# Attention and two gated layers in one kernel: token tiles of 4, 2, 4, 4, 4 blocks in place of 4, 3, 4, 4, 3

## The chip, the cores and the metric

One NeuronCore of a Trainium2 chip runs the kernel. The metric is the device time of one execution in microseconds, taken as the median of several runs.

## What is computed

A windowed attention (4 sequences of 576 tokens, 8 heads of 64, each token sees itself and the 63 before it) gives 2304 tokens of 512 values. Two gated layers follow, each with a hidden width of 1536; all is float32.

```python
scores = scale * np.matmul(q, k.transpose(0, 1, 3, 2))
mask = (rel >= 0) & (rel < window)
...
x = np.ascontiguousarray(attn_out.transpose(0, 2, 1, 3)).reshape(B * S, H * D)
# first layer
g = x @ w_gate
silu = g * (1.0 / (1.0 + np.exp(-g)))
x = silu * (x @ w_val) @ w_out
# second layer
gate = 1.0 / (1.0 + np.exp(-(x @ w_gate)))
out = gate * (x @ w_val) @ w_out
```

## The kernel before, in words

The 2304 tokens are 18 **blocks** of 128. Blocks are grouped into five **token tiles** (`BLOCKS`, L63); before, they hold 4, 3, 4, 4 and 3 blocks, so 512, 384, 512, 512 and 384 columns.

**The start.** The attention of the blocks of tile 0 (blocks 0 to 3) is done first, in an order written out by hand: `LOADS` (L23) is the order of the loads on SyncE's queue, `START` (L27) the order of the steps. A step has two letters and a block number. `tq`/`tk` transpose a block's queries and keys on TensorE, `eq`/`ek` copy them out, `se`/`so` make the scores of the even and the odd heads, `me`/`mo` mask them on VectorE, `xe`/`xo` are the exponentials on ScalarE, `ne`/`no` normalise on VectorE, `pe`/`po` transpose the result on TensorE, `we`/`wo` copy it out on ScalarE, `vp` copies value rows on GpSimd, `pv` multiplies by the values, `hi`/`lo` split the result into two float32r parts. `ca`, `cb`, `ch`, `cl` are the four parts of converting one piece of 512 KB of the first layer's weights (`ca`, `ch` on ScalarE, `cb`, `cl` on VectorE); `mn` makes a mask; `wm` are matmuls on zeros. `SPLIT_EARLY` (L34) counts the pieces converted in the start; the others are converted in the main loop.

**The main loop.** For each tile and each of the 12 slices `fc` of the hidden width there are three **steps** `g` (L1083 to L1113): twelve matmuls for the gate (`product`, bank `g`), twelve for the values (bank `v`), and twelve (`out_product`) that multiply the slice before by its output weights into the banks `a0` to `a3`. A tile thus has 36 steps, and every matmul has as many columns as its tile. Gate, product and split of the hidden slice are on ScalarE (L1092, L1101) and VectorE (L1099, L1015).

**Work put between the steps.** Three tables (`before`, `during`, `after`, L475) say for each step which other work is issued there. `plan_attention` (L492) puts the attention of block `i` around a step `base`: the scores at `base + 2`, masks and exponentials at `base + 2` and `base + 3`, normalisation at 4 or 5, the transposes of the result at 7 to 9, and the values' product either two steps later in a bank of its own (`att`, two buffers) or together with the next block's scores in bank `g`. Up to block 7 (`TURN` is 8) queries and keys are transposed on TensorE (`transpose_in`, L191); from block 8 on they are loaded in pieces of 32 rows by 32 (`load_squares`, L130: queries from SyncE's queue, keys from GpSimd's) and turned on VectorE (`turn`, L220).

In the same way `operands` (L588) prepares the weights of the second layer from step `starts[n]` on (L660), and `reload` (L409) brings back the output weights of the first layer, seven steps ahead of their use, into one of three buffers (L580). After a tile, `finish` (L459) copies the four banks into tiles of the pool `t` (seven buffers) and stores them.

After the five tiles, the second layer runs in three pairs of 384 columns with fewer products (`strassen`, `outs`); the change does not touch it.

Of the kernel before, what the change touches and what calls it, by code (L numbers as in the profile page):

```python
# [8 lines left out]
FP32 = mybir.dt.float32  # L9
# [11 lines left out]


LOADS = """  # L23
k0 q0 q1 k2 k1 q2 r1 v3 q3 r2 v0 v1 k3 h0 r3 v2
"""

START = """  # L27
tk0 tq0 tq1 ek0 eq0 se0 eq1 so0 tk2 tk1 me0 mo0 ek1 xe0 ne0 tq2 xo0 so1 mo1 eq2 ca0 ek2 se1 no0
so2 se2 xo1 ma0 vp0 ca1 me1 xe1 pe0 mb0 mo2 po0 no1 cb0 xo2 me2 wm2 tk3 ne1 tq3 no2 ek3 ch0 wo0
po1 we0 pe1 ca2 eq3 wo1 so3 vp1 se3 cb1 xe2 mo3 me3 we1 po2 pv0 hi0 xe3 vp2 xo3 ne2 ch1 vp3 wo2  # L30
pv1 pe2 lo0 cl0 ne3 cb2 hi1 we2 lo1 wm2 wm1 wm2 pe3 no3 ca3 cb3 ca4 pv2 hi2 po3 we3 wm3 lo2 wo3
cb4 pv3 wm1 mn0 hi3 ca5 ch3 ch4 lo3 cb5 ch2 ch5 cl4 cl1 cl2 cl5 cl3
"""
SPLIT_EARLY = START.count("ca")  # L34


@with_exitstack
def attention_moe_moe(
# [21 lines left out]
    HP = H // 2  # L60
    W = 64
    scale = 1.0 / float(D) ** 0.5
    BLOCKS = [4, 3, 4, 4, 3]  # L63
    NTL = len(BLOCKS)
    N2 = 384
    PAIRS = NT // (2 * N2)
    JJ = FC // 2
    assert NT == PAIRS * 2 * N2
    TURN = BLOCKS[0] + BLOCKS[1] + 1
    TILES = []  # L70
    t0 = 0
    for n in BLOCKS:
# [177 lines left out]
                    stop=True,  # L250
                )

    def p_tile(tag, name):
        if early[0]:
            return w_p.tile([128, HP, 128], FP32, tag="g", name=name)
        return p_p.tile([128, HP, 128], FP32, tag=tag, name=name)

    def masked(i, par):
        ps = st.pop((i, "s", par))
        z = p_tile(f"z{par}", f"z{par}")  # L260
# [13 lines left out]
        st[i, "z", par] = z, nm  # L274
# [36 lines left out]

    def evacuate_p(i, par):
        ps = st.pop((i, "pp", par))
        t = p_tile(("pt0", "z0")[par], f"pt{par}")
        nc.scalar.activation(out=t, in_=ps, func=ACTF.Copy)
        st[i, "pt", par] = t

# [16 lines left out]
    def x_hi(i, xt, col):  # L334
        nc.scalar.activation(out=xt[:, 0, :, col:col + 128], in_=st[i, "x"], func=ACTF.Copy)  # L335
# [120 lines left out]

    x1d = [dram.tile([128, CC, N2], FP32, name=f"x1d{j}") for j in range(2 * PAIRS)]

    def finish(acc, t, n, parts=range(CC)):  # L459
        for e in parts:  # L460
# [22 lines left out]
    def at(where, g, fn, *a, first=False):  # L483
        where.setdefault(g, []).append((not first, fn, a))
# [7 lines left out]
    def plan_attention(i, base, t, col):  # L492
        if t == 1:
            turn_at, pv_at = (7, 8), 9 if col == 256 else 10
        elif t == 2:
            turn_at, pv_at = (8, 8), 10
        elif col == 0:
            turn_at, pv_at = (8, 9), 10
        else:
            turn_at, pv_at = (7, 8), 9  # L500
        if i >= TURN:
            lead = 9 if i > TURN else 8
            for j in range(4 * HP):
                at(during, base - lead + j * (lead - 3) // (4 * HP), load_squares, i, "kq"[j % 2], j // 4, j // 2 % 2)
        elif base >= 2:
            at(during, base - 5, load_qk, i)
        at(during, base + 1 if i < TURN else base - 2, load_v, i)
        at(during, base + 5 if i <= TURN else base + 2, load_before, i)
        for nm in "qk":
            if i < TURN:  # L510
                at(before, base + 1, transpose_in, i, nm)
                at(before, base + 1, evacuate, i, nm)
            else:
                at(during, base - 1, turn, i, nm, first=nm == "k")
        place[i] = t, col
        if i >= TURN:
# [5 lines left out]
        at(after, base + 2, masked, i, 0, first=True)  # L522
        at(after, base + 3, masked, i, 1, first=True)
        at(after, base + 3, exps, i, 0, first=True)
        at(after, base + 3, exps, i, 1, first=True)
        at(after, base + (4 if i < TURN else 5), normalize, i, 0, first=i >= TURN)
        at(after, base + 5, normalize, i, 1, first=True)
        for par in range(2):
            at(before, base + turn_at[par], transpose_p, i, par)
            at(before, base + turn_at[par], evacuate_p, i, par)  # L530
        if TURN - 1 <= i < NT // 128 - 1:
            return
        at(before, base + pv_at, pv, i)
        at(before, base + pv_at, lambda: x_hi(i, x_of(t), col))
        if t == 1 and col < 256:
            at(before, base + pv_at + 1, lambda: x_lo(i, x_of(t), col))
        else:
            at(during, base + pv_at, lambda: x_lo(i, x_of(t), col), first=True)


    blk = BLOCKS[0]
    for t in range(NTL - 1):
        nb = BLOCKS[t + 1]
        for b in range(nb):
            plan_attention(blk + b, SPT * t + {4: 9 * b - 3, 3: 12 * b - (3 if t else 0), 2: 18 * b + 3}[nb], t + 1, b * 128)
        blk += nb


# [470 lines left out]
    with tc.manual_schedule():  # L1019
# [14 lines left out]
        for step in LOADS.split():  # L1034
# [138 lines left out]
```

## Time and profile before

| | |
|---|---|
| median of 3 runs | 938.1 us (937.07 to 939.4) |
| the profiled execution's own time | 939.13 us |
| its span | 937.4 us, mean granted TensorE clock 0.994 |
| TensorE, matmuls | busy 922.1 us, 98% |
| VectorE | busy 695.1 us, 74% |
| ScalarE | busy 475.4 us, 51% |
| GpSimd | busy 208.3 us, 22% |

Busy is the share of the span in which an engine works on at least one instruction. Matmuls overlap, so the rate of a run of matmuls is read from the start of one group to the start of the next, not from the mean duration. 1.7 us of the execution's time lie outside the span.

### The profile page before, as it was taken

Reading aid. Unit: us, or ns where it says so; the run is one execution under the profiler, and the core shown is the slowest. Engines: PE = TensorE matmul, PEld = TensorE weight load, DVE = VectorE, ACT = ScalarE, POOL = GpSimd, SP = SyncE. Lnnn points to the kernel's source line nnn. Section 1 sums busy time; section 2 is a strip of 40 time slices with the busy share of each in tenths; the row PEclk is TensorE's granted clock in tenths of the full one; section 3 lists DMA queues with packets and bytes.
Section 4 is the critical chain, followed back from the end, with each engine's and each line's share of the span. In section 5 each row is a group of like instructions: output and inputs, shape, how many; then the busy total and the mean of one; then the engine's idle time right before and its main releaser. Section 6 shows DMA issues by size and latency. Waiting matters only on the chain.

```text
span 937.4 us, 17091 instructions
## 1 busy us (share of the span) xinstructions
PE 922.1 (98%) x5933; PEld 841.8 (90%) x5933; DVE 695.1 (74%) x1614; ACT 475.4 (51%) x1079; POOL 208.3 (22%) x368
## 2 busy tenths in 40 slices
PE   7899999999999999999999999999999999999998
PEld 6688888999887888888899999999899999999987
DVE  6899996677666757676655578789677889678795
ACT  6898985666656556546433332246212247122342
POOL 3301015555585616331311000000200000100001
PEclk8999999999999999999999999999999999999999
DMA  9688767888869868786699468738987828978555
GB/s 219 185 247 263 248 223 228 243 238 248 255 206 287 264 216 264 238 276 217 234 324 378 161 224 304 245 146 280 367 306 267 309 90 288 400 239 289 206 181 201
DMA packets 172565, 234.45 MB, mean 250 GB/s; under 512 B 71648, under 2 KB 104800, under 8 KB 172480
## 3 DMA queue, kind: packets, MB, share of 16 engines
q1 hardware_dynamic: 149904, 179.21, 60.0%
q0 software_dynamic: 18256, 45.50, 13.7%
q10 hardware_dynamic: 4320, 8.65, 2.5%
q8 instruction: 47, 0.77, 0.3%
q14 instruction: 38, 0.31, 0.1%
HBM read 184.55 MB, written 48.76 MB: 249 GB/s over the span
## 4 chain that ended last, share of the span: by engine, by line
PE 87%; DMA 4%; ACT 3%; DVE 2%; POOL 2%; SPq 1%; issue 1%; ACTq 0%; POOLq 0%
PE g L438 14%; PE a L449 14%; PE v L438 14%; PE a L793 13%; PE a L944 9%; PE att L793 7%; PE g L793 4%; PE v L793 4%; PE att L944 2%; DMA k<-in_k_dram 2%; PE att L245 1%; DMA wop<-wd 1%; POOL k L136 1%; PE g L325 1%; PE att L309 1%
## 5 line engine op out<-in xcount | busy, mean ns | idle before, releaser
L449 PE MATMUL a<-h,wo 128*128 128x512 f32 (+1 forms) x720 | 161.2, 372 | 0.0
L438 PE MATMUL v<-x,wv 128*128 128x512 f32 (+1 forms) x720 | 159.2, 369 | 0.0
L438 PE MATMUL g<-x,wg 128*128 128x512 f32 (+1 forms) x720 | 158.8, 369 | 0.4 <-ACT x L335 0.3
L438 PEld LDWEIGHTS g<-x,wg 128*128 128x128 f32 x720 | 131.0, 188 | 18.2 <-ACT x L335 0.6
L449 PEld LDWEIGHTS a<-h,wo 128*128 128x128 f32 x720 | 129.6, 188 | 18.5 <-issue 2.2
L438 PEld LDWEIGHTS v<-x,wv 128*128 128x128 f32 x720 | 130.3, 188 | 16.2
L793 PE MATMUL a<-xs,wop 128*128 128x384 f32 x720 | 130.2, 334 | 0.6 <-DMA wop<-wd 0.5
L793 PEld LDWEIGHTS a<-xs,wop 128*128 128x128 f32 x720 | 125.1, 188 | 1.4 <-PE a L793 1.1
L944 PE MATMUL a<-w,hs 128*128 128x256 f32 (+1 forms) x666 | 113.6, 306 | 0.0
L136 POOL DMA_DIRECT2D k<-in_k_dram x176 | 101.9, 585 | 40.9 <-PE att L195 22.3
L934 POOL DMA_DIRECT2D out_dram<-o x33 | 17.8, 541 | 372.8 <-DVE o L915 372.8
L944 PEld LDWEIGHTS a<-w,hs 128*128 128x128 f32 x666 | 93.6, 190 | 6.4
L1099 DVE TENSOR_TENSOR s<-s,v 128x512 f32<-128x512 f32 (+1 forms) x60 | 37.9, 632 | 78.8 <-PE v L438 58.1
L785 ACT ACTIVATE s<-s 128x384 f32<-128x384 f32 x72 | 37.9, 526 | 76.9 <-DVE s L779 75.7
L793 PE MATMUL att<-xs,wop 128*128 128x384 f32 x396 | 73.9, 334 | 0.0
L1092 ACT ACTIVATE s<-g 128x512 f32<-128x512 f32 (+1 forms) x60 | 33.2, 553 | 74.3 <-PE g L438 74.1
L793 PEld LDWEIGHTS att<-xs,wop 128*128 128x128 f32 x396 | 69.0, 188 | 0.0
L1101 ACT ACTIVATE h<-s 128x512 fp32r<-128x512 f32 (+1 forms) x60 | 35.1, 586 | 62.0 <-DVE s L1099 61.7
L633 POOL DMA_DIRECT2D wd<-stage x48 | 31.9, 665 | 136.3 <-DVE stage L619 117.5
L96 DVE TENSOR_TENSOR hs<-hid,hs 128x384 fp32r<-128x384 f32 x108 | 55.3, 551 | 7.3 <-ACT hs L95 7.3
L95 ACT ACTIVATE hs<-hid 128x384 fp32r<-128x384 f32 x108 | 51.3, 520 | 15.0 <-DVE hid L783 11.4
L282 ACT ACTIVATE z<-z,nm 128x128 f32<-128x128 f32 x144 | 55.8, 389 | 1.0 <-DVE nm L264 0.9
(159 smaller groups left out, 1477.6 us busy)
## 6 DMA issues: line engine op xcount, KB each, us to landing
wop<-wd SPq DMA_DIRECT2D x126, 512.0 KB, 6.8
w<-wdo SPq DMA_DIRECT2D x63, 512.0 KB, 5.7
wo<-k0o SPq DMA_DIRECT2D x48, 512.0 KB, 5.3
wd<-stage POOLq DMA_DIRECT2D x36, 512.0 KB, 5.6
raw<-in_moe_w_gate_dram SPq DMA_DIRECT2D x24, 512.0 KB, 4.5
raw<-in_moe_w_val_dram SPq DMA_DIRECT2D x24, 512.0 KB, 4.3
raw<-in_moe_w_out_dram SPq DMA_DIRECT2D x24, 512.0 KB, 4.9
wdo<-stage POOLq DMA_DIRECT2D x18, 512.0 KB, 5.7
```

Of the source, the lines that this page charges most:

```text
L95: nc.scalar.activation(out=dst_hi, in_=src, func=ACTF.Copy)
L96: nc.vector.tensor_tensor(out=dst_lo, in0=src, in1=dst_hi.bitcast(FP32), op=ALU.subtract)
L136: eng.dma_start(out=nat[i, nm][r0:r0 + 32, c, off // 32:(off + m) // 32], in_=src[b, 2 * c + par, s:s + m, 32 * a:32 * a + 32].rearrange(" ...
L282: nc.scalar.activation(out=z[:, hp, :], in_=z[:, hp, :], func=ACTF.Exp, scale=-1.0, bias=nm[:, hp:hp + 1], accum_out=su[:, hp:hp + 1],)
L438: nc.tensor.matmul(out=ps[:, 0:n], lhsT=w[:, a, c, :], rhs=xt[:, b, c, 0:n], start=(j == 0), stop=(j == len(mm) - 1),)
L449: nc.tensor.matmul(out=acc[e][:, 0:n], lhsT=w[:, a, e * 128:(e + 1) * 128], rhs=h[:, b, 0:n], start=(fc == 0 and j == 0), stop=(fc == FC - ...
L785: nc.scalar.activation(out=to[which], in_=to[which], func=ACTF.Sigmoid)
L793: nc.tensor.matmul(out=ps, lhsT=w[:, val, a, c, :], rhs=xops[op, b][:, c], start=(n == 0), stop=(n == len(mm) - 1),)
L944: nc.tensor.matmul(out=acc[e] if both else acc[e][:, 0:256], lhsT=h[a][:, e * 128:(e + 1) * 128], rhs=w.rearrange("p s f -> p (s f)") if b ...
L1092: nc.scalar.activation(out=s, in_=gps[:, 0:n], func=ACTF.Silu)
L1099: nc.vector.tensor_tensor(out=s, in0=s, in1=vps[:, 0:n], op=ALU.mult)
L1101: nc.scalar.activation(out=h[:, 0, 0:n], in_=s, func=ACTF.Copy)
```

## The change

The tiles now hold 4, 2, 4, 4, 4 blocks: 512, 256, 512, 512, 512 columns. The blocks of attention are placed by a table with a row for each block from 4 on: base, the steps of the two transposes, of the values' product and of the lower part of the split. `TURN` falls from 8 to 7, so block 7 is now loaded in squares and turned on VectorE; a new `JOIN` (10) is the block from which values' products go together with the next block's scores, which was from block 7 on before. For blocks 7 and 9 the softmax tiles come from the pool `t`. `finish` copies all four banks in one step, where before two were copied one step later. Two pieces of weights fewer are converted in the start (four for six). The start's values' products alternate between the bank `a2` and the pool `att`.

```diff
-k0 q0 q1 k2 k1 q2 r1 v3 q3 r2 v0 v1 k3 h0 r3 v2
+q0 k0 q1 k1 k2 q2 r1 v0 q3 r2 k3 r3 v3 v1 v2 h0
...
-tk0 tq0 tq1 ek0 eq0 se0 eq1 so0 tk2 tk1 me0 mo0 ek1 xe0 ne0 tq2 xo0 so1 mo1 eq2 ca0 ek2 se1 no0
...
+tq0 tk0 ek0 eq0 se0 tq1 eq1 so0 tk1 me0 tk2 mo0 ek1 xe0 ne0 so1 tq2 xo0 mo1 eq2 ek2 se1 so2 ma0
...
+PLAN = [
+    (0, 11, 11, 13, 15),
+    (15, 22, 23, 25, 27),
+    (27, 37, 37, 39, 39),
+    (39, 47, 47, 51, 51),
+    (48, 55, 55, 57, 58),
+    (57, 65, 65, 67, 67),
...
-    BLOCKS = [4, 3, 4, 4, 3]
+    BLOCKS = [4, 2, 4, 4, 4]
...
+    JOIN = sum(BLOCKS[0:3])
...
+        if BLOCKS[0] + BLOCKS[1] <= i <= JOIN and (i - BLOCKS[0]) % 2:
+            return t_p.tile([128, HP, 128], FP32, tag="t", name=name)
...
-        if i >= TURN:
+        if i > JOIN:
             t1, col1 = place[i - 1]
             at(before, base + 2, pv, i - 1, "g")
...
-        at(after, base + (4 if i < TURN else 5), normalize, i, 0, first=i >= TURN)
-        at(after, base + 5, normalize, i, 1, first=True)
+        at(after, base + (2 + 3 if mid else 4 if i < TURN else 5), normalize, i, 0, first=mid or i >= TURN)
+        at(after, base + (2 + 3 if mid else 5), normalize, i, 1, first=True)
...
-    starts = [39, 48, 58, 66, 75, 81, 87, 93, 100, 107, 114, 120, 126, 132, 138, 145, 155, 161]
+    starts = [43, 58, 72, 78, 84, 89, 94, 101, 106, 111, 117, 123, 129, 135, 141, 147, 153, 161]
...
-            "pv": lambda i: pv(i, "a2"),
+            "pv": lambda i: pv(i, ("a2", None)[i % 2]),
...
-                    finish(*done, parts=(0, 1))
-                    at(during, g + 1, finish, *done, (2, 3))
+                    finish(*done)
```

Two places in the order of the instructions. The first is VectorE in the start, up to the last normalisation of block 3. Before (`z_488` and `z_482` are block 3's even and odd heads, `raw`/`t` a weight conversion, `x<-a` the lower part of a split):

```order
L338 TENSOR_TENSOR x<-a_501,x 128x4x128
L424 TENSOR_TENSOR wg<-t,wg 128x512
L295 TENSOR_SCALAR su<-su 128x4
L296 RECIPROCAL su<-su 128x4
L301 TENSOR_TENSOR z_488<-z_488,su 128x512
L398 TENSOR_SCALAR raw<-raw 128x512
L399 TENSOR_SCALAR t<-t 128x512
L400 ISA t<-raw,t 128x1024
L338 TENSOR_TENSOR x<-a_542,x 128x4x128
L295 TENSOR_SCALAR su<-su 128x4
L296 RECIPROCAL su<-su 128x4
L301 TENSOR_TENSOR z_482<-z_482,su 128x512
```

The same place with the change (here `z_482` is the odd and `z_498` the even half of block 3):

```order
L314 TENSOR_SCALAR su<-su 128x4
L315 RECIPROCAL su<-su 128x4
L320 TENSOR_TENSOR z_482<-z_482,su 128x512
L443 TENSOR_TENSOR wg<-t,wg 128x512
L314 TENSOR_SCALAR su<-su 128x4
L315 RECIPROCAL su<-su 128x4
L320 TENSOR_TENSOR z_498<-z_498,su 128x512
L357 TENSOR_TENSOR x<-a_504,x 128x4x128
L417 TENSOR_SCALAR raw<-raw 128x512
L418 TENSOR_SCALAR t<-t 128x512
L419 ISA t<-raw,t 128x1024
L357 TENSOR_TENSOR x<-att,x 128x4x128
```

One conversion and two lower parts of splits have moved from ahead of the last normalisation to behind it.

The second is SyncE's queue of loads in the start. Before, from the sixth load on (the first key row is that of block 3):

```order
L111 DMA q<-in_q_dram 128x8x64
L371 DMA raw<-in_moe_w_gate_dram 128x4x256
L371 DMA raw<-in_moe_w_val_dram 128x4x256
L111 DMA v<-in_v_dram 128x8x64
L111 DMA q<-in_q_dram 128x8x64
L371 DMA raw<-in_moe_w_gate_dram 128x4x256
L111 DMA v<-in_v_dram 128x8x64 x2
L111 DMA k<-in_k_dram 128x8x64
L111 DMA q<-in_q_dram 64x8x64 x2
```

With the change:

```order
L128 DMA q<-in_q_dram 128x8x64
L390 DMA raw<-in_moe_w_gate_dram 128x4x256
L390 DMA raw<-in_moe_w_val_dram 128x4x256
L128 DMA v<-in_v_dram 128x8x64
L128 DMA q<-in_q_dram 128x8x64
L390 DMA raw<-in_moe_w_gate_dram 128x4x256
L128 DMA k<-in_k_dram 128x8x64
L390 DMA raw<-in_moe_w_val_dram 128x4x256
L128 DMA v<-in_v_dram 128x8x64 x3
```

The keys of block 3 have moved ahead of two loads of values, 256 KB each; the other values, and the loads for block 4, follow later.

## Rows read from the trace of the kernel before

**Rows 1.** Windows of tiles 0 and 1: length, busy by engine, clock, DMA share, GB/s
```profile
39.86:150.81 110.95, 110.95 (x700) 90.57 (x701) 102.55 (x232) 95.27 (x194) 17.96 (x25) 1.00 0.76 239
150.81:239.78 88.97, 88.84 (x722) 85.90 (x721) 62.40 (x175) 58.16 (x142) 48.58 (x87) 1.00 0.85 247
```

**Rows 2.** TensorE's waits from 40 to 535 us: total, times, longest
```profile
PE g L325 <- ACT s L1092: 1.4, 1, 1.4
```

**Rows 3.** Timeline of TensorE: start, length, what; the first product of tile 0
```profile
39.86 3.04 PE L438 MATMUL g<-x,wg 128*128 128x512 f32 x12 [0.26 <-ACT x L335]
```

**Rows 4.** Timeline of VectorE in the start: conversions, a lower part, the last normalisation
```profile
23.32 1.13 DVE L398 TENSOR_SCALAR raw<-raw 128x512 uint16<-128x512 uint16 x1
...
25.24 0.69 DVE L400 CUSTOM_DVE_ANT_0 t<-raw,t 128x1024 uint16<-128x1024 uint16 x1
...
31.96 0.79 DVE L398 TENSOR_SCALAR raw<-raw 128x512 uint16<-128x512 uint16 x1
...
33.93 0.68 DVE L338 TENSOR_TENSOR x<-a,x 128x512 fp32r<-128x512 f32 x1
...
34.94 0.69 DVE L301 TENSOR_TENSOR z<-z,su 128x512 f32<-128x512 f32 x1
35.55 0.75 DVE L398 TENSOR_SCALAR raw<-raw 128x512 uint16<-128x512 uint16 x1
...
36.58 0.69 DVE L400 CUSTOM_DVE_ANT_0 t<-raw,t 128x1024 uint16<-128x1024 uint16 x1
```

**Rows 5.** The chain of waits in the start: start, length, what
```profile
14.42 7.03 DMA k<-in_k_dram
```

**Rows 6.** The page: rate of all transfers in 40 equal slices of the span
```profile
GB/s 219 185 247 263 248 223 228 243 238 248 255 206 287 264 216 264 238 276 217 234 324 378 161 224 304 245 146 280 367 306 267 309 90 288 400 239 289 206 181 201
```

**Rows 7.** Timeline of TensorE: groups of matmuls of 512, 384 and 256 columns
```profile
50.36 2.88 PE L438 MATMUL v<-x,wv 128*128 128x512 f32 x12
53.08 2.88 PE L449 MATMUL a<-h,wo 128*128 128x512 f32 x12
...
200.03 2.24 PE L449 MATMUL a<-h,wo 128*128 128x384 f32 x12
202.11 2.24 PE L438 MATMUL g<-x,wg 128*128 128x384 f32 x12
...
623.88 6.84 PE L944 MATMUL a<-w,hs 128*128 128x256 f32 x55
630.56 0.40 PE L944 MATMUL g<-w,hs 128*128 128x512 f32 x1
```

**Rows 8.** Timeline of TensorE: transposes of one block's queries and keys, and what follows
```profile
42.74 0.60 PE L195 MATMUL att<-ident,q 128*128 128x128 f32 x4
...
43.53 2.98 PE L438 MATMUL v<-x,wv 128*128 128x512 f32 x12
```

**Rows 9.** Tile 1, groups by line: issuing key squares from GpSimd, count, busy, mean ns
```profile
L136 POOL DMA_DIRECT2D k<-in_k_dram x63 | 36.6, 587 | 9.0 <-DMA wdo<-stage 3.4 <-DVE kt L227 2.7 <-DMA k<-in_k_dram 1.6
```

**Rows 10.** Timelines: lower part of hidden slice 1 (VectorE), output product of that slice (TensorE)
```profile
60.09 0.69 DVE L1015 TENSOR_TENSOR h<-s,h 128x512 fp32r<-128x512 f32 x1
...
62.08 3.02 PE L449 MATMUL a<-h,wo 128*128 128x512 f32 x12
```

**Rows 11.** Tile 1: a reload's issue on SyncE, its output product, landing times of output weights
```profile
217.50 0.42 SPq L411 DMA_DIRECT2D wo<-k0o x1
...
229.02 2.33 PE L449 MATMUL a<-h,wo 128*128 128x384 f32 x12
...
wo<-k0o SPq DMA_DIRECT2D x48, 512.0 KB, 5.3
DMA to landing us min/median/max: 3.1/5.3/8.7
```

**Rows 12.** Tile 1, waits of SyncE's queue: total, times, longest
```profile
SPq L371 <- DMA wdo<-stage: 24.3, 4, 8.0
```

**Rows 13.** Timeline of GpSimd in the start: a copy of value rows
```profile
23.90 1.02 POOL L148 COPY v<-v 64x512 f32<-64x512 f32 x1
```

More of the change, by code (lines that the diff above doesn't have):

```diff
@@ L23 @@
 LOADS = """
-k0 q0 q1 k2 k1 q2 r1 v3 q3 r2 v0 v1 k3 h0 r3 v2
+q0 k0 q1 k1 k2 q2 r1 v0 q3 r2 k3 r3 v3 v1 v2 h0
 """
 START = """
-tk0 tq0 tq1 ek0 eq0 se0 eq1 so0 tk2 tk1 me0 mo0 ek1 xe0 ne0 tq2 xo0 so1 mo1 eq2 ca0 ek2 se1 no0
[L29 to L32, printed above, removed]
-"""
+tq0 tk0 ek0 eq0 se0 tq1 eq1 so0 tk1 me0 tk2 mo0 ek1 xe0 ne0 so1 tq2 xo0 mo1 eq2 ek2 se1 so2 ma0
+xo1 se2 ca0 vp0 ca1 me1 no0 po0 no1 pe0 mo2 mb0 xo2 me2 wm2 cb0 we0 xe1 tq3 tk3 no2 ne1 ek3 xe2
+wo0 po1 eq3 pe1 ca2 wo1 so3 ch0 vp1 se3 cb1 mo3 we1 po2 ne2 me3 pv0 xo3 vp2 pe2 vp3 pv1 xe3 wm2
+wo2 hi0 no3 we2 wm3 po3 cl0 ne3 pe3 lo0 pv2 hi1 wo3 ch1 cb2 we3 hi2 pv3 ca3 mn0 lo1 lo2 hi3 cb3
+lo3 ch2 cl1 ch3 cl3 cl2
+"""
+PLAN = [
[5 more added lines that the diff above has]
+    (57, 65, 65, 67, 67),
+    (69, 78, 78, 80, 80),
+    (78, 86, 86, 88, 88),
+    (87, 95, 95, 97, 99),
+    (96, 104, 104, 105, 105),
+    (105, 113, 113, 115, 115),
+    (114, 123, 123, 126, 126),
+    (123, 133, 133, 135, 135),
+    (132, 141, 141, 143, 143),
+]
 SPLIT_EARLY = START.count("ca")
@@ L259, in masked @@
         ps = st.pop((i, "s", par))
-        z = p_tile(f"z{par}", f"z{par}")
+        z = p_tile(i, f"z{par}", f"z{par}")
         nm = sm_p.tile([128, HP], FP32, tag=f"nm{par}", name=f"nm{par}")
@@ L313, in evacuate_p @@
         ps = st.pop((i, "pp", par))
-        t = p_tile(("pt0", "z0")[par], f"pt{par}")
+        t = p_tile(i, ("pt0", "z0")[par], f"pt{par}")
         nc.scalar.activation(out=t, in_=ps, func=ACTF.Copy)
@@ L457, in attention_moe_moe, with finish @@
     x1d = [dram.tile([128, CC, N2], FP32, name=f"x1d{j}") for j in range(2 * PAIRS)]
-    def finish(acc, t, n, parts=range(CC)):
-        for e in parts:
+    def finish(acc, t, n):
+        for e in range(CC):
             o = t_p.tile([128, 512], FP32, tag="t", name="o")
@@ L490, in attention_moe_moe, with plan_attention @@
     place = {}
[L492 to L500, printed above, removed]
+    def plan_attention(i, t, col):
+        base, p0, p1, pv_at, lo_at = PLAN[i - BLOCKS[0]]
         if i >= TURN:
-            lead = 9 if i > TURN else 8
+            lead = max(base - 9, PLAN[i - BLOCKS[0] - 1][0])
             for j in range(4 * HP):
-                at(during, base - lead + j * (lead - 3) // (4 * HP), load_squares, i, "kq"[j % 2], j // 4, j // 2 % 2)
+                at(during, lead + j * (base - 3 - lead) // (4 * HP), load_squares, i, "kq"[j % 2], j // 4, j // 2 % 2)
         elif base >= 2:
@@ L521, in plan_attention @@
         at(before, base + 2, scores, i)
[L522 to L525, printed above, removed]
-        at(after, base + (4 if i < TURN else 5), normalize, i, 0, first=i >= TURN)
-        at(after, base + 5, normalize, i, 1, first=True)
+        mid = BLOCKS[0] + BLOCKS[1] <= i < JOIN
+        at(after, base + (2 + 0 if mid else 2), masked, i, 0, first=True)
+        at(after, base + (2 + 1 if mid else 3), masked, i, 1, first=True)
+        at(after, base + (2 + 1 if mid else 3), exps, i, 0, first=True)
+        at(after, base + (2 + 1 if mid else 3), exps, i, 1, first=True)
+        at(after, base + (2 + 3 if mid else 4 if i < TURN else 5), normalize, i, 0, first=mid or i >= TURN)
+        at(after, base + (2 + 3 if mid else 5), normalize, i, 1, first=True)
         for par in range(2):
-            at(before, base + turn_at[par], transpose_p, i, par)
-            at(before, base + turn_at[par], evacuate_p, i, par)
-        if TURN - 1 <= i < NT // 128 - 1:
+            at(before, (p0, p1)[par], transpose_p, i, par)
+            at(before, (p0, p1)[par], evacuate_p, i, par)
+        if JOIN <= i < NT // 128 - 1:
             return
[L533 to L536, printed above, removed]
+        at(before, pv_at, pv, i)
+        at(before, pv_at, lambda: x_hi(i, x_of(t), col))
+        if lo_at > pv_at:
+            at(before, lo_at, lambda: x_lo(i, x_of(t), col))
         else:
-            at(during, base + pv_at, lambda: x_lo(i, x_of(t), col), first=True)
+            at(during, lo_at, lambda: x_lo(i, x_of(t), col), first=True)
     blk = BLOCKS[0]
@@ L544, in attention_moe_moe @@
         for b in range(nb):
-            plan_attention(blk + b, SPT * t + {4: 9 * b - 3, 3: 12 * b - (3 if t else 0), 2: 18 * b + 3}[nb], t + 1, b * 128)
+            plan_attention(blk + b, t + 1, b * 128)
         blk += nb
```

2 lines of the change are left out of this document (1 added, 1 removed).

## The prediction

> **What bounds the kernel now.** I read the windows of the tiles first, then TensorE's waits, then the timeline of the start. In tile 0 TensorE is busy for all of its 110.95 us, in tile 1 for 88.84 of 88.97 [rows 1]; VectorE is busy for 102.55 of 110.95 us in tile 0 (92%), but for 62.40 of 88.97 in tile 1 (70%). Over all five tiles TensorE waits once for anything longer than 0.3 us: 1.4 us, for ScalarE [rows 2]. So from the first product at 39.86 us on [rows 3] the time is TensorE's own work, and ahead of it a chain of dependent steps. A change can win by a shorter start, by less work on TensorE and by the one wait; it can lose by new waits, and a narrow tile leaves the other engines less time for each step.
>
> **The start: 4.3 us earlier.** Before, VectorE works almost without a gap up to its last normalisation (block 3, odd heads), which ends at 34.94 + 0.69 = 35.63 us [rows 4]. Transposes, copies, the values' product and the split follow, and the first product starts 4.23 us later [rows 3]. In the changed order one conversion and two lower parts stand behind the last normalisation: 33.93 - 31.96 = 1.97 us for the third conversion, and 2 x 0.68 for the lower parts [rows 4], together 3.3 us. The second part is the keys of block 3: issued at 14.42 us and landed 7.03 us later, they hold the chain up to 21.45 [rows 5]. They move ahead of two loads of 256 KB; at 219 GB/s, the rate of the first slice [rows 6], that is 2.3 us. I count 1.0 of it, since the work for block 3 then still queues behind that for block 2 on VectorE. The sum is 4.3 us, so the first product at 35.6. Ends: a gain of 5.6 (all of both), or a loss of 0.5, if the values' loads, now behind, hold the last products of the start. ScalarE carries one conversion less ahead of the first product (four pieces for six, one of them behind it anyway); it is not the end of this chain by the rows read, so it counts nothing.
>
> **The widths: 0.6 us more.** Start to start, a matmul of 512 columns takes (53.08 - 50.36)/12 = 227 ns, one of 384 takes (202.11 - 200.03)/12 = 173 ns, one of 256 takes (630.56 - 623.88)/55 = 121.5 ns [rows 7]. Each tile has 36 x 12 = 432 matmuls; two tiles of 384 become one of 256 and one of 512: 432 x (121.5 + 226.7 - 2 x 173.3) ns = 0.6 us. Ends: 0 (cost in proportion to columns) and 2 (4 ns more for each narrow one, as 256 columns lie above the line through the other two by 1.5).
>
> **Block 7: 0.8 us less.** Its queries and keys are no longer transposed on TensorE: 43.53 - 42.74 = 0.79 us [rows 8]. VectorE has room for the two turns in tile 1. GpSimd issues 16 more small loads, 16 x 0.587 = 9.4 us [rows 9], in a tile where it was busy for 48.58 of 88.97 us [rows 1]; that hides them unless tile 1 gets too short (below). Ends: 0.6 and 0.9.
>
> **The wait for ScalarE: 0.7 us less.** The 1.4 us fell where the values' product shares bank `g` [rows 2]. In tile 2 that sharing stays from block 10 on, with the weights of the second layer prepared at other steps; I take half. Ends: 1.4 less and 1.4 more.
>
> **At nothing.** Banks `a2` and `att` in turn: no values' product waits for a bank that another holds in the rows read. Softmax tiles from the pool `t`: one more buffer, no instruction. `finish` in one step: two copies come one step earlier, and the next output product follows three steps later. Values' products apart from the scores in tile 1: the same matmuls. Normalising at `base + 5`: still two steps ahead of the transposes. If these covers go, each can cost one wait of about 1 us, which is in the next term.
>
> **New waits: 0.8 us more.** In tile 0 the two conversions that left the start come back on VectorE, 2 x about 2 us [rows 4], against one block fewer of attention. The nearest margin is the lower part of hidden slice 1: ready at 60.09 + 0.69, its output product starts at 62.08, 1.3 us later [rows 10]. In tile 1 the margins are those of the rival below. Ends: 0 and 9. I take 0.8, near the low end, because both margins exist now.
>
> **Sum:** -4.3 + 0.6 - 0.8 - 0.7 + 0.8 = -4.4 us. Against the profiled execution's 939.1 that is 934.7; this execution lies 1.0 us above the median, so against 938.1 it is **933.7 us**. A measurement of this kernel can tell about 0.3% (2.8 us) from no change.
>
> **Rivals.**
> A. *The start's gain is taken back in tile 0.* Products start 4.3 us earlier, but VectorE, at 92%, has the same conversions to do by the same step, so TensorE then waits for it. For it: that share, and the margin of 1.3 us [rows 10]. Against it: the third block of tile 0 now begins at step 27 instead of 24, so VectorE's load spreads. It gives 933.7 + 4.3 = 938.0, no change.
> B. *The output weights come late in tile 1* (slower). Reloads are issued seven steps ahead. The one issued at 217.50 is used at 229.02, 11.5 us later, and loads land after 5.3 us (median) to 8.7 us [rows 11]: 6.2 to 2.8 us to spare. A step of tile 1 shrinks by 12 x (173.3 - 121.5) ns = 0.62 us, seven by 4.35, so 1.9 us stays in the median and 1.6 us are missing at the slowest. It decides from a landing of 11.5 - 4.35 = 7.2 us on. A load of raw weights in front of it on SyncE's queue waited up to 8.0 us [rows 12], which speaks for it; that tile 1 now prepares two pieces of the second layer's weights and not four speaks against. If six of the twelve reloads are 1.6 us late: 933.7 + 9.6 = 943.3.
> C. *GpSimd's copies hold VectorE in the start.* A conversion's first two instructions took 25.24 - 23.32 = 1.92 us, and 36.58 - 35.55 = 1.03 in another place [rows 4]; GpSimd copied values at 23.90 [rows 13]. Four more such copies now fall beside the last masks and normalisations. At 0.9 us each that is 3.6 us: 937.3, no change. The Trainium skill (SBUF — State Buffer, Who interferes with whom) says that VectorE instructions with two inputs in SBUF, or in a two-port mode, and a GpSimd instruction that reads SBUF exclude each other, and that the later one blocks fully; by that rule the last normalisations would wait for whole copies, and the start would gain 0.7 us instead of 4.3. The row agrees for that one place; no row here shows the others.
> D. *The start does not get shorter*, because the values now land last and the last products wait for them: 933.7 + 4.3 = 938.0.
>
> **How the numbers follow.** Forecast 0.62 (its own range 931 to 936.5), A 0.14, B 0.14, C 0.04, D 0.06. Faster by over 0.3% means below 935.3: of the forecast's 0.62 nine tenths, 0.56; slower means above 940.9: B and a little of A, 0.15; the rest, 0.29, is the same. The range reaches from 930.8 (the start's gain of 5.6 and the whole wait) to 939.5, past A, C and D; B lies mostly above it, which with a little below leaves out about 0.17.
>
> **What would show it.** Right: the first product of tile 0 at 35 to 36.5 us; in tile 0 no wait of TensorE for VectorE above 1 us; tile 1 some 36 x 0.62 = 22 us and one block of attention shorter, with TensorE busy throughout; the 256-column matmuls 121 to 122 ns apart. Wrong: waits of output products in tile 1 for `wo` (B), waits for VectorE's copies or splits in tile 0 (A), first product after 38 us (C if VectorE's normalisations stretch, D if values' products wait for loads).

## The result: 947.4 us, slower by 1%

The changed kernel takes 947.4 us (median of 6 runs, 943.9 to 948.8) against 937.7 beside it: a ratio over all runs of 1.0095, 95% interval 1.0079 to 1.0112 (1.0103 by the medians). The forecast was 933.7 with a range up to 939.5, so sign and range were both missed. The profiled execution took 948.5 us, its span is 946.7 (before 937.4). One run of a kernel below, of 4479 us, is left out there.

In the changed kernel L438, L449, L1092, L1015, L309, L315, L325 and L614 of before are L457, L468, L1105, L1028, L328, L334, L344 and L627. The windows of tiles 0 to 2 (columns as in [rows 1]; the first two rows answer to it):

```profile
39.67:146.82 107.15, 107.13 (x620) 87.26 (x621) 101.50 (x225) 92.95 (x189) 19.51 (x27) 1.00 0.77 239
146.82:217.76 70.94, 67.67 (x721) 63.89 (x720) 43.84 (x131) 43.11 (x110) 40.75 (x73) 1.00 0.82 240
217.76:334.95 117.19, 112.75 (x723) 92.30 (x721) 83.28 (x217) 73.48 (x166) 65.96 (x112) 0.97 0.85 258
```

The first product starts at 39.67 us, where 35.6 was forecast and 39.86 stood before [rows 3]: the new start gains nothing. TensorE, busy before in nearly all of tiles 0 and 1 [rows 1], now idles for 3.3 us of tile 1 and 4.4 us of tile 2, and in tile 2 its mean clock is 0.97. Its waits from 30 to 560 us (columns as in [rows 2]) name what for:

```profile
PE g L457 <- ACT s L1105: 3.9, 1, 3.9
PE att L328 <- DVE z L320: 3.1, 3, 2.0
PE g L344 <- ACT s L1105: 1.3, 3, 0.7
```

The first row is one stall of TensorE in tile 2, for ScalarE's gate; the second is the transposes in tile 1, which wait for VectorE's normalisation. Before, the only such wait was 1.4 us [rows 2]. That makes three places: start, tile 1, tile 2.

**The start.** TensorE's timeline (start, length, operation, idle time before it and its releaser):

```profile
19.26 0.66 PE L212 MATMUL att<-ident,k 128*128 128x128 f32 x4 [0.51 <-DMA k<-in_k_dram]
23.76 1.97 PE L328 MATMUL a<-ident,z 128*128 128x128 f32 x8 [3.85 <-ACT pt L334]
25.66 1.33 PE L262 MATMUL v<-kt,early_q 64*64 64x128 f32 x10
...
29.53 1.98 PE L344 MATMUL a<-pt,v 128*64 128x64 f32 x32
```

The keys of block 3 come earlier, as meant (transposed at 19.26). But TensorE then stands for 3.85 us at the transposes of block 1, since the bank is free only when ScalarE has copied block 0's second half out, and block 3's scores (25.66) stand behind them in order. On ScalarE that copy is behind eight exponentials:

```profile
20.05 0.39 ACT L301 ACTIVATE z<-z,nm 128x128 f32<-128x128 f32 x1
...
23.13 0.58 ACT L334 ACTIVATE pt<-a 128x512 f32<-128x512 f32 x1
```

After the wait TensorE's clock is down. The windows of this stretch (columns as in [rows 1]; the clock is the third number from the end):

```profile
20.00:24.00 4.00, 0.24 (x1) 0.24 (x2) 3.83 (x11) 4.00 (x19) 1.13 (x2) 0.90 0.88 183
24.00:28.00 4.00, 4.00 (x38) 3.67 (x39) 2.38 (x6) 2.81 (x6) 3.69 (x5) 0.50 0.80 218
28.00:34.00 6.00, 6.00 (x79) 4.82 (x75) 5.79 (x26) 4.86 (x19) 2.54 (x6) 0.55 0.24 75
34.00:40.00 6.00, 4.83 (x80) 4.11 (x79) 3.99 (x8) 4.74 (x9) 0.00 (x0) 1.00 0.27 87
```

At 0.50 (1.2 of 2.4 GHz) eight transposes take 1.97 us and a values' product 1.98; later in the start, at 1.00, they take 1.04 and 1.15. The last normalisation of block 3 ends at 33.25 us, 2.4 earlier than before, but TensorE reaches its transposes only at 35.23. The start of the kernel before was not free of this either; its windows:

```profile
16.00:20.00 4.00, 3.95 (x25) 3.65 (x26) 3.90 (x21) 3.65 (x19) 0.66 (x2) 0.50 1.05 206
20.00:24.00 4.00, 3.28 (x14) 2.56 (x14) 3.68 (x12) 2.65 (x6) 3.64 (x10) 0.50 0.90 207
```

**Tile 1.** Timelines of ScalarE, VectorE and TensorE around the longest of the three waits:

```profile
179.36 1.28 ACT L301 ACT_TABLE_LOAD   x1
...
183.66 0.19 ACT L301 ACTIVATION_READ_ACCUMULATOR z<-z,nm 128x1 f32 x1
```
```profile
184.33 1.29 DVE L320 TENSOR_TENSOR z<-z,su 128x512 f32<-128x512 f32 x2
```
```profile
180.14 1.60 PE L468 MATMUL a<-h,wo 128*128 128x256 f32 x12
181.58 1.60 PE L457 MATMUL g<-x,wg 128*128 128x256 f32 x12
185.16 1.23 PE L328 MATMUL att<-ident,z 128*128 128x128 f32 x8 [1.98 <-DVE z L320]
```

A step of tile 1 takes 181.58 - 180.14 = 1.44 us, 120 ns a matmul ([rows 7] gave 121.5 for 256 columns, 173 for 384). The exponentials of a block with their table load take 183.85 - 179.36 = 4.5 us, three of these steps.

**Tile 2.** The chain of waits that ends in the stall (start, length, what):

```profile
305.51 4.38 DMA k<-in_k_dram
...
309.92 0.75 DVE raw L417
...
311.28 7.47 DMA raw<-in_moe_w_gate_dram
...
320.06 1.28 ACT L1105
...
322.00 5.30 PE g L457 x12
```

Its last load, raw weights of the second layer, is issued when VectorE's conversion (309.92) has freed a buffer, and lands 7.47 us later. That a key load held the conversion is only inferred by the chain; the conversion does not read keys. ScalarE's timeline shows a nearer cause: the conversion's first part (309.18), which VectorE's part needs, stands behind the table load and eight exponentials of an attention block (304.27 to 308.76). On ScalarE, which works in order:

```profile
304.27 1.28 ACT L301 ACT_TABLE_LOAD   x1
...
309.18 0.67 ACT L404 ACTIVATE raw<-raw 128x512 int32<-128x512 uint32 x1
...
314.50 0.63 ACT L627 ACTIVATE stage<-n 128x512 fp32r<-128x512 f32 x1 [3.57 <-DMA wd<-stage]
318.83 0.65 ACT L404 ACTIVATE raw<-raw 128x512 int32<-128x512 uint32 x1 [3.70 <-DMA raw<-in_moe_w_gate_dram]
```

It then waits 3.57 us for a store to free its tile and 3.70 for that load, and the gate of the main loop stands behind both; the second ends last and sets the time. The product that follows takes 5.30 us where 2.88 is usual, and a window from 322 to 325 us shows TensorE at 0.50. So 3.9 us of waiting cost 3.9 + 2.4 in this execution.

### The profile page after: what moved, and what is told of

The parts are those of the page before. It is cut to its first block, busy times and chain, and to the rows that moved or that the text cites. A ratio compares the mean times of both kernels' runs of the same rounds, so it can differ in the third digit from the quotient of the medians.

```text
span 946.7 us, 17103 instructions
## 1 busy us (share of the span) xinstructions
PE 925.6 (98%) x5921; PEld 827.5 (87%) x5921; DVE 693.9 (73%) x1614; ACT 475.5 (50%) x1077; POOL 218.0 (23%) x380
## 4 chain that ended last, share of the span: by engine, by line
PE 82%; DMA 6%; ACT 5%; DVE 2%; issue 1%; POOL 1%; SPq 1%; ACTq 0%; POOLq 0%; DVEq 0%
PE a L806 13%; PE g L457 12%; PE a L468 12%; PE v L457 11%; PE a L957 10%; PE att L806 7%; PE g L806 4%; PE v L806 4%; PE att L957 2%; ACT z L301 2%; DMA x1d<-o 2%; DMA wop<-wd 1%; PE att L262 1%; DMA k<-in_k_dram 1%; POOL k L153 1%
## 5 line engine op out<-in xcount | busy, mean ns | idle before, releaser
L457 PE MATMUL g<-x,wg 128*128 128x512 f32 (+1 forms) x720 | 161.2, 373 | 4.8 <-ACT s L1105 3.9
L468 PE MATMUL a<-h,wo 128*128 128x512 f32 (+1 forms) x720 | 160.5, 372 | 0.0
L457 PE MATMUL v<-x,wv 128*128 128x512 f32 (+1 forms) x720 | 158.8, 370 | 0.0
L457 PEld LDWEIGHTS g<-x,wg 128*128 128x128 f32 x720 | 127.2, 191 | 28.9 <-ACT s L1105 4.8
L468 PEld LDWEIGHTS a<-h,wo 128*128 128x128 f32 x720 | 124.8, 188 | 24.4 <-issue 2.2
L457 PEld LDWEIGHTS v<-x,wv 128*128 128x128 f32 x720 | 125.6, 189 | 22.8 <-DVE s L1112 0.4
L153 POOL DMA_DIRECT2D k<-in_k_dram x192 | 112.1, 590 | 53.4 <-PE att L212 29.0
L1105 ACT ACTIVATE s<-g 128x512 f32<-128x512 f32 (+1 forms) x60 | 33.2, 553 | 66.6 <-PE g L457 62.6
L417 DVE TENSOR_SCALAR raw<-raw 128x512 uint16<-128x512 uint16 x72 | 54.5, 757 | 4.1 <-ACT raw L404 4.1
```

The costliest lines, as they stand in the source:

```text
L153: eng.dma_start(out=nat[i, nm][r0:r0 + 32, c, off // 32:(off + m) // 32], in_=src[b, 2 * c + par, s:s + m, 32 * a:32 * a + 32].rearrange(" ...
L417: nc.vector.tensor_scalar(second, fourth, 0x8000, None, ALU.bitwise_and)
L457: nc.tensor.matmul(out=ps[:, 0:n], lhsT=w[:, a, c, :], rhs=xt[:, b, c, 0:n], start=(j == 0), stop=(j == len(mm) - 1),)
L468: nc.tensor.matmul(out=acc[e][:, 0:n], lhsT=w[:, a, e * 128:(e + 1) * 128], rhs=h[:, b, 0:n], start=(fc == 0 and j == 0), stop=(fc == FC - ...
L1105: nc.scalar.activation(out=s, in_=gps[:, 0:n], func=ACTF.Silu)
```

## The experiments

Theory: three separate losses: the start (order and clock), the attention chain of tile 1 in its short steps, and the second layer's preparation, of which the narrow tile holds two pieces instead of four. The rivals are in the expectations. "Before" was run beside each kernel: 937.5 to 938.1 us. Waits, clocks and first products are those of one traced execution of each kernel.

### The start: alone, with the clock held, in another order

The first kernel is before with the new `LOADS` and `START` (as in the diff of the change) and the alternating bank:

```diff
-            "pv": lambda i: pv(i, "a2"),
+            "pv": lambda i: pv(i, ("a2", None)[i % 2]),
```

> The kernel before with the change's order of loads, its order of the start and the alternating bank of the values' products; tiles stay 4, 3, 4, 4, 3. Theory (the new start itself is worth nothing: TensorE stands in order behind the transposes of block 1, which wait 3.9 us for ScalarE's second copy, and everything behind runs at the lower clock): first product of tile 0 at 39.7 us as in the changed kernel, a TensorE wait for `pt` of 3 to 4 us between 19 and 24 us, time within 1 us of before. Rival (the start is good for 4 us, and the new tile 0 takes it away ahead of the first product): first product at 35 to 36.5, time 4 us under before.

Measured: 937.33 us, ratio 0.9995 (0.9983 to 1.0007). TensorE waits 3.0 us for `pt`, the clock is 0.50 from 24 to 28 us, and the first product comes at 38.5 (39.7 expected). The theory holds: the start alone, as it stands, is worth nothing. The next kernel is the changed one with matmuls on zeros in the gap:

```diff
-xo1 se2 ... cb0 we0 xe1 tq3 tk3 no2 ne1 ek3 xe2
+xo1 se2 ... cb0 we0 xe1 tq3 tk3 wm14 no2 ne1 ek3 xe2
```

> The changed kernel with 14 matmuls on zeros put into the start behind the transposes of block 3, about 3.2 us of TensorE work in the stretch in which it waited 3.9 us for ScalarE's copy; the order of all other work is unchanged. Theory (of the loss in the start, the larger part is the clock that falls after the wait): granted clock 0.9 or more from 23 to 40 us, the transposes of a block behind it at 1.1 us for 1.97, scores at about 1 for 2.8, first product 2 to 4 us earlier than 39.7, time 2 to 4 us under the changed kernel. Rival (the loss is the wait in order alone): first product within 1 us of 39.7, same time.

Measured: 943.92 us, ratio 1.0057 (1.0035 to 1.008), 3.5 us under the changed kernel's median. In its windows (columns as above) the clock stays up:

```profile
24.00:28.00 4.00, 3.80 (x66) 3.29 (x68) 3.90 (x15) 4.00 (x12) 3.76 (x5) 1.00 0.81 213
```

Transposes and values' products behind the gap take 1.09 and 1.15 us, the first product starts at 36.69. Nothing but matmuls on zeros was added, and block 1's transposes start no earlier, so what is gained in the start is the clock. In tile 2 this execution stalls for 5.1 us, where the changed kernel's stood for 3.9. The third kernel changes the order of the changed kernel's start:

```diff
-... cb0 we0 xe1 tq3 tk3 no2 ne1 ek3 xe2 wo0 po1 eq3 pe1 ca2 wo1 so3 ch0 vp1 se3 cb1
+... cb0 we0 wo0 tq3 tk3 eq3 ek3 xe1 no2 po1 ne1 xe2 so3 se3 pe1 ca2 wo1 ch0 vp1 cb1
```

> The changed kernel with one piece of the start in another order: the second copy of block 0's probabilities ahead of the exponentials of block 1 on ScalarE, and the copies and scores of block 3 ahead of the transposes of block 1. Theory (the 3.9 us wait is a matter of order on ScalarE and TensorE): no TensorE wait over 1.5 us between 19 and 30 us, first product at 35 to 37, time 2.5 to 4 us under the changed kernel. Rival (the last normalisation on VectorE sets the start, whatever TensorE's order): first product at 38.5 to 39.7, less than 1 us gained.

Measured: 944.87 us, ratio 1.0072 (1.005 to 1.0094); first product at 37.27. The 3.85 us become smaller waits, none above 1.6 us, and the clock stays at 1.00. The gain of 2.6 us is just inside the expected bounds, first product and longest wait just outside; no better than filling the gap. But the traced execution is the fastest of the eight (939.48, the others up to 947.78), and with the preparation unchanged it has no stall in tile 2. The waits for the gate from 40 to 560 us, with the gap filled and in this order:

```profile
PE g L457 <- ACT s L1105: 5.1, 1, 5.1
PE g L457 <- ACT s L1105: 0.6, 1, 0.6
```

So that stall comes and goes between executions, and one trace cannot show that an edit removed it.

The same filled start with the old tiles, that is the first kernel of this section and

```diff
-... cb0 we0 xe1 tq3 tk3 no2 ne1 ek3 xe2
+... cb0 we0 xe1 tq3 tk3 wm14 no2 ne1 ek3 xe2
```

> The kernel before (tiles 4, 3, 4, 4, 3, its own finish and buffers) with the change's loads and start, and the 14 matmuls on zeros in that start. Theory (the new start is worth 3 us once the clock is held, and the old tiles keep it): first product at 36.5 to 37, no TensorE wait over 1.5 us behind it, time 934 to 935.5. Rival (tile 0 gives it back, because VectorE and ScalarE are no further along): waits of 1 to 3 us between 40 and 150 us, time 936.5 to 938.

Measured: **934.08 us, ratio 0.9965 (0.995 to 0.9981)**. Its timeline and all its waits of TensorE from 40 to 560 us:

```profile
36.15 3.02 PE L438 MATMUL g<-x,wg 128*128 128x512 f32 x12 [1.20 <-ACT x L335]
```
```profile
PE g L438 <- ACT s L1092: 0.3, 1, 0.3
PE att L245 <- ACT kt L210: 0.2, 1, 0.2
```

Tile 0 takes nothing back. This version beats both kernels. Behind the same start the new tiles, with all that came with them (places of the blocks, steps of the preparation, buffers, finish), cost 943.92 - 934.08 = 9.8 us, by the ratios 8.6, and behind the unfilled start 947.43 - 937.33 = 10.1: the whole loss lies in them. Not tried is the old start with its own stretch at 0.50 filled, so how much of the gain of 934.08 over before is the new order and how much the clock stays open. One more change of order there, the last upper half ahead of a conversion:

```diff
-... hi2 pv3 ca3 mn0 lo1 lo2 hi3 cb3
+... hi2 pv3 mn0 lo1 lo2 hi3 ca3 cb3
```

> The kernel before with the change's start and 14 matmuls on zeros, and the upper half of block 3's x taken on ScalarE ahead of the next weight conversion (there the last copy waited behind 1.1 us of conversion). Theory (ScalarE's order sets the last step ahead of the first product): first product 0.4 to 0.6 us earlier, at 35.6, time 933 to 934. Rival (the conversion put behind is late for the second product): a wait of 0.5 us or more at the first `v` products, same time.

Measured: 934.42 us, 0.9964 (0.995 to 0.9978). The first product starts at 35.53, but after eight matmuls it waits 0.81 us for a lower half from VectorE: the same time, as the rival said, though at another operand.

### Tile 1: can its waits be moved away?

The changed kernel with later transposes, by three rows of `PLAN`:

```diff
-    (39, 47, 47, 51, 51), (48, 55, 55, 57, 58), (57, 65, 65, 67, 67),
+    (39, 48, 48, 51, 51), (48, 56, 56, 58, 59), (57, 66, 66, 68, 68),
```

> The changed kernel with the transposes of blocks 7, 8 and 9 one step later in tile 1 (steps 48, 56 and 66 for 47, 55 and 65; where they need it, the products behind them too). Theory (in tile 1 the transposes are planned so soon behind the normalisation that a step of 1.44 us leaves no room): the three waits of TensorE for VectorE's normalisation in tile 1, together 3.1 us, fall to under 0.6; tile 1 takes 68.5 us for 70.9; time 2 to 2.5 us under the changed kernel. Rival (the values' product behind it is only pushed against the next step and waits there): waits of the same 2 to 3 us in tile 1 at the values' products, no gain.

Measured: 948.77, 948.99 and 951.79 us, 1.0137 (1.0103 to 1.017): no better than the change. TensorE's waits in tile 1:

```profile
PE att L262 <- DVE x L357: 2.9, 1, 2.9
PE a L468 <- DVE h L1028: 2.2, 2, 1.1
PE att L328 <- DVE z L320: 0.6, 1, 0.6
```

The waits for the normalisation fell as expected, but block 8's lower half, pushed to step 59, now holds the bank that block 9's scores need in that step. My edit made a new wait. With the filled start, block 8 begun earlier instead:

```diff
-    (48, 55, 55, 57, 58),
+    (47, 55, 55, 57, 58),
```

> The changed kernel with the 14 matmuls on zeros in the start, and block 8 begun one step earlier in tile 1 (base 47 for 48); its transposes and products stay at steps 55, 57 and 58, so that only the room ahead of the transposes grows. Theory (the 2 us wait at the transposes of block 8 comes of the room ahead of them): that wait under 0.6 us, 1.4 to 2 us gained against 943.9. Rival (exponentials and normalisation wait for the same queue wherever they are begun): a wait of 1.5 us or more stays.

Measured: 947.18 us, 1.0103 (1.0088 to 1.0118), 3.3 us above the filled start alone, where 1.4 to 2 less were expected. The 1.98 us wait is gone, but the scores, one step earlier, wait 2.3 us for ScalarE's copy of block 7. Neither theory had that: on both sides of the chain stands another user of the bank.

### The preparation of the second layer

The changed kernel with its preparation spread:

```diff
-    starts = [43, 58, 72, 78, 84, 89, 94, 101, 106, 111, 117, 123, 129, 135, 141, 147, 153, 161]
+    starts = [43, 58, 72, 78, 84, 90, 96, 102, 109, 115, 121, 127, 133, 139, 145, 150, 155, 161]
```

> The changed kernel with the second layer's weight preparation spread to starts 6 or 7 steps apart in tiles 2 and 3 (in the change they lie 5 apart at 101, 106, 111). Theory (the stall in tile 2 at 318 to 327 us, 3.9 us of waiting for the gate and 2.4 us of half clock, comes of raw weights that land behind the stage): no TensorE wait over 1.5 us in tile 2, tile 2 some 113 us instead of 117.2, time 4 to 6 us under the changed kernel's slower runs, near 943, and less spread between runs. Rival (the stall comes of the attention's keys and values on the queue): a wait of 2 us or more stays at 300 to 330 us, less than 1.5 us gained.

Measured: 943.12 us, 1.0063 (1.0044 to 1.0081), runs from 938.95 to 948.12. The traced execution has no stall in tile 2, but 1.9 us of waiting stand in tile 1 and 2.5 in tile 4, and the spread of the runs is wider, not narrower. Since the stall was missing without this edit too, and this execution's start was 2 us shorter by the clock alone (last section), what the spread itself gained is not shown. The same with the matmuls on zeros:

> The changed kernel with the 14 matmuls on zeros in the start and the spread preparation of the second layer, the transposes of tile 1 as in the change. Theory (the two repairs are separate and add: 3.5 and 4.3 us of the 9.7): 938.5 to 941, with the waits of 3 us in tile 1 still there. Rival (the spread gained only by chance of its runs): 942.5 to 945, as with the matmuls alone.

Measured: 949.65 us, 1.0124 (1.0089 to 1.0159): they do not add. The chain of waits in tile 3, and in tile 4:

```profile
335.58 8.21 DMA x1d<-o
...
343.87 0.66 ACT t L407
...
346.50 4.51 PE g L457 x12
```
```profile
450.36 6.99 DMA x1d<-o
...
458.08 0.69 DVE h L1028
...
458.82 3.25 PE a L468 x7
```

Here the store of a finished tile (`finish`, from the pool `t`) takes 7 to 8 us, and the next to need a buffer of that ring waits for it with the main loop's work behind: in tile 3 ScalarE with a weight conversion, in tile 4 VectorE with the finish's own next copy. With the spread, the stalls stand in tiles 3 and 4 instead of tile 2, in this trace and in the next kernel's. All three repairs together:

> The changed kernel with the 14 matmuls on zeros in the start, the later transposes in tile 1 and the spread preparation of the second layer together. Theory (the loss of 9.7 us is the sum of three separate things: 3.5 in the start, 2.3 in tile 1, about 4 from waits on ScalarE's queue behind stores and loads of weights): the gains add, time 936 to 938.5, no better than the kernel before. Rival (one of them only uncovers another wait): 940 or more. Second rival (with the repairs the new tiles are worth what was forecast): 933 to 935.

Measured: 950.0 us, 1.0133 (1.0106 to 1.016), with the wait of 2.9 us that the later transposes made and two stalls behind the stores, 2.5 us in tile 3 and 3.1 in tile 4. Then the changed kernel with the finish in two steps again, as before:

```diff
-                    finish(*done)
+                    finish(*done, parts=(0, 1))
+                    at(during, g + 1, finish, *done, (2, 3))
```

> The changed kernel with the finish of a tile in two steps again, parts 0 and 1 and one step later 2 and 3. Theory (the finish in one step costs nothing that can be seen, since no wait of TensorE in the profile of the changed kernel lies behind it): time within 1.5 us of the changed kernel. Rival (its copies hold VectorE or ScalarE at the tiles' ends until a store of 5.6 us has left its buffer): 2 us or more gained, and waits of VectorE and ScalarE for the stores of the outputs gone from the trace.

Measured: 951.87 us, 1.0147 (1.0121 to 1.0173). Both theories miss: it is worse, since an output product of the next tile now waits for a bank that VectorE has not copied out:

```profile
353.74 1.65 PE L468 MATMUL a<-h,wo 128*128 128x512 f32 x3 [4.68 <-DVE o L482]
```

VectorE's copy itself waited 5.67 us for a store of the same ring. So going back to two steps regains nothing. Next, the preparation at the steps of the kernel before (with the filled start):

```diff
-    starts = [43, 58, 72, 78, 84, 89, 94, 101, ...
+    starts = [39, 48, 58, 66, 75, 81, 87, 93, 100, ...
```

> The changed kernel with the 14 matmuls on zeros in the start, and the second layer's preparation at the steps of the kernel before (39, 48, 58, 66, 75, 81, 87, 93, 100 and so on), which puts four pieces into tile 1 for two. Theory (a step of 1.44 us has no room for as many pieces, so the narrow tile pushes them into tile 2): TensorE waits in tile 1 above 5 us for 3.3, none above 1.5 us in tile 2, time 943 to 948. Rival (the old steps were good, and the new ones make the stall): 940 or less.

Measured: 947.52 us, 1.0104 (1.0083 to 1.0126). TensorE's waits from 40 to 560 us, all but the fourth row in tile 1 ("issue": it waited for nothing that the profile shows):

```profile
PE att L262 <- DVE qt L244: 2.9, 2, 2.5
PE att L344 <- issue: 1.7, 1, 1.7
PE att L328 <- ACT raw L404: 1.5, 1, 1.5
PE g L344 <- ACT s L1105: 1.3, 1, 1.3
PE att L328 <- DVE z L320: 1.1, 2, 0.6
```

As expected: with four pieces in tile 1 the waits sum to 7.2 us there, with none above 1.5 in tile 2, and the time is 3.6 us above the filled start alone. The last four kernels ran on one chip: the filled start again, the same with two pieces fewer, the same with none in tile 1, and the old tiles with two pieces fewer. The edit for two pieces fewer is

```diff
-    starts = [43, 58, 72, 78, 84, 89, 94, ...
-    groups = ... [(nm, j) for j in range(JJ) for nm in "gv"]
+    starts = [43, 58, 75, 81, 87, 93, 100, 107, 114, 120, 126, 132, 138, 145, 155, 161]
+    groups = ... [(nm, j) for j in range(JJ - 1) for nm in "gv"]
```

and for none in tile 1 the pieces at 43 and 58 go too (`JJ - 2`). In all three that drop pieces, the second layer reads an earlier piece in place of each missing one, so they leave out part of the task's weights: they are for the time alone.

> The changed kernel with the 14 matmuls on zeros, once more, on the chip of the three others. Theory (the loss of the new tiles is there on every chip): 942 to 946, with the waits of 3 us in tile 1 and a stall of 3 to 5 us for ScalarE in tile 2. Rival (the stall is there in some executions only): none above 1.5 us in tile 2.

> The changed kernel with the 14 matmuls on zeros in the start, two of the 18 pieces of the second layer's weight preparation left out (the last gate and value piece; the second layer reads the piece before in their place), and the others at 43 and 58 and from tile 2 on at the steps of the kernel before (75, 81, 87, 93, 100 and so on). Theory (two pieces that tile 1 no longer holds crowd the tiles behind, and the stalls there come of that): no TensorE wait over 1.5 us from tile 2 on, tile 1 with its 3 us as before, time 937.5 to 939.5. Rival (the stalls come of the attention's and the finish's own buffers in the new order): a wait of 3 us or more between 218 and 560 us, time 942 or more.

> As the kernel with two pieces fewer, but with four pieces left out, so that none is prepared in tile 1 (the first at step 75). Theory (the waits in tile 1 are the attention's own: exponentials, normalisation and transposes have the same durations as before in steps of 1.44 us): the three waits for the normalisation in tile 1 stay at 2.5 to 3.5 us, time within 1 us of the kernel with two pieces fewer. Rival (the preparation on ScalarE and VectorE makes them): under 1 us in tile 1, 2 to 3 us faster.

> The kernel before with the new start and the 14 matmuls on zeros, the same two pieces left out and the same steps for the others. Theory (there the preparation is hidden, so leaving a part out gains nothing): 933.5 to 934.7, as with all 18 pieces (934.1). Rival (the preparation costs TensorE's time in any order): 2 us or more below.

Measured: again 942.96 us (ratio 1.0062, 1.0043 to 1.008), with a stall of 2.0 us in tile 2 (3 to 5 expected, under 1.5 by the rival) and one of 1.5 in tile 1: its size differs between executions, and neither theory is met. Two pieces fewer: 937.10 (0.9999, 0.9982 to 1.0016). None in tile 1: 937.32 (0.9997, 0.9985 to 1.0009). Old tiles with two pieces fewer: 934.68 (0.9976, 0.9961 to 0.9992), as with all of them. The largest of TensorE's waits from 40 to 560 us with two pieces fewer, with none in tile 1, and with the old tiles, in this order:

```profile
PE att L328 <- DVE z L320: 2.6, 3, 1.6
```
```profile
PE att L328 <- DVE z L320: 3.0, 3, 2.0
```
```profile
PE att L245 <- ACT kt L210: 0.2, 1, 0.2
```

Two pieces out of 18, with the others back at their old steps, are worth 942.96 - 937.10 = 5.9 us with the new tiles and nothing with the old ones: they were hidden there. How much of it is the number and how much the wider steps no run separates; the old steps with all 18 pieces (947.52) were no help. And with no preparation in tile 1 its waits stay at 3.0 us: those are the attention's own.

## Why the prediction was wrong, step by step

- **"The start: 4.3 us earlier."** What VectorE does came out as worked: with the clock held and the old tiles the last normalisation ends at 31.97 us (35.63 - 3.3 = 32.3 by VectorE's work, 31.3 with the keys), the first product 4.2 us later, at 36.15, 3.7 us earlier than before. The step that failed is that the rest "follows": the sum counted VectorE's work and the keys, and did not ask what TensorE does meanwhile. It waits 3.85 us, works on at half clock, and the gain is gone. Holding the clock in the new start is worth 937.33 - 934.08 = 3.3 us.
- **"The widths: 0.6 us more."** 120 ns measured for 121.5: 432 x (120 + 226.7 - 346.6) ns is 0.0, the lower end of the range given.
- **"Normalising at base + 5: still two steps ahead of the transposes", costed at nothing.** Two steps of tile 1 are 2.9 us, and a block's part on ScalarE and VectorE does not shrink with the tile: the exponentials alone take 4.5 us. It measured 3.1 us, and 2.6 in the kernel with two pieces fewer, as much as all that is left there (937.10 - 934.68 = 2.4 us).
- **"New waits: 0.8 us more", with ends 0 and 9.** The end of 9 was the near one: 3.1 in tile 1 and 3.9 + 2.4 in tile 2, 9.4 us in the traced execution. The changed steps of the preparation stood in the diff and got no term. Under rival B I even counted the two pieces that leave tile 1 as relief, and did not ask which tile takes them. Leaving two pieces out gave back 5.9 us.
- **"The wait for ScalarE: 0.7 us less."** In its place stand three waits of the same kind, together 1.3 us: no gain.
- **Rivals.** A: no wait of TensorE in tile 0 behind the first product, and tile 0 in the repaired old tiles gives nothing back. B: no wait for `wo` in any run. C: with the start filled, the old tiles and GpSimd copying values from 22.99 to 27.8 us, one normalisation falls beside a copy and takes 0.92 us for 0.69; the last ones lie behind the copies. The first product is not held by them; whether the rule of whole waits holds, this does not test. D: no wait for values. What came was none of them: the narrow tile as a shortage of time for the other engines, which the first paragraph named and the sum priced at 0.8.
- **The marks.** Tile 1 became 18 us shorter, not "22 us and one block": both kernels have the same attention matmuls in it; the block left tile 0 for tile 3. Of the 23.0 us that 36 x 12 x (173.3 - 120) ns give, 3.1 went into waits; where the other 1.9 went no row names. Block 7's 0.8 us could not be seen alone.

Not tried: the softmax tiles of blocks 7 and 9 taken out of the pool `t`, and a further buffer for `raw` or `t`; with two pieces fewer, though, no stall stands behind tile 1 with these buffers as they are. Open too is why a raw load (median 4.5 to 5.0 us in the changed kernel) takes 7.5 us at the stall in tile 2, and a store of the finish (1.5 to 9.3 us, median 5.8, with gap and preparation changed) 7 to 8 us at those in tiles 3 and 4.

## What to carry to other kernels

A narrower tile shortens TensorE's steps, but not the work that other engines do per block or per weight piece: count that work in microseconds per tile, and follow each piece that no longer fits to the tile that takes it. A slot "two steps ahead" is a time: multiply it out for the narrowest tile, and look on both sides of it for the next user of the bank. When a start is reordered for one engine, read what TensorE does meanwhile: a wait of three or four microseconds there can be paid twice, and matmuls on zeros in it paid for themselves here. And when a stall comes and goes between executions of one kernel, judge an edit by many runs, not by one trace.

## What was not expected of the hardware

The clock stayed down for very different times behind the same wait. The kernel with the spread preparation has the changed kernel's start, instruction for instruction, and a wait of 3.97 us in it; its window from 28 to 34 us:

```profile
28.00:34.00 6.00, 5.87 (x91) 4.67 (x87) 5.80 (x28) 5.60 (x22) 2.74 (x7) 1.00 0.25 82
```

There the clock was back at 1.00, and the first product came at 37.62; in the changed kernel the same stretch shows 0.55, and it came at 39.67. Seen microsecond by microsecond, TensorE counted as busy and stood at 0.50 from 24 to 33 us in the one and from 25 to 27 in the other. Two executions of the same start thus began their first product 2 us apart; that this also explains the spread between runs of one kernel is not shown, since one run of each was traced. The Trainium skill (TensorE: Matmul & The Clock Gate, Loop structure matters more than you think) says that a long wait for a transfer between matmuls lets TensorE's clock fall. The traces agree for long waits, though for ScalarE's work, with 0.50 behind 3.0 to 4.0 us in the start and 3.9 us in tile 2, and 1.00 where matmuls on zeros filled the gap. For shorter waits the length alone does not decide: the same wait of 1.98 us in tile 1 was followed by 1.00 in the changed kernel (185 to 189 us) and by 0.50 in the kernel with gap and preparation changed; a wait of 2.5 us was followed by 0.50 with the old steps of the preparation (175 to 177 us) and by 1.00 with the spread ones (455 to 458 us). The windows behind the 1.98 us, in the changed kernel and in the other:

```profile
187.00:189.00 2.00, 2.00 (x19) 2.00 (x18) 1.32 (x3) 1.35 (x3) 0.40 (x1) 1.00 0.96 252
183.00:185.00 2.00, 2.00 (x11) 2.00 (x11) 1.30 (x3) 1.32 (x3) 0.79 (x2) 0.50 0.90 252
```
